# DMA transposes against TensorE transposes with token-major copies, half-width broadcast tiles and a deeper chunk order in a transformer block's forward and backward pass

## The chip, the cores and the metric

The kernel runs on one core of a Trainium2 chip. A core has a matrix engine (TensorE, PE in the profile; its weight loads are PEld), a vector engine (VectorE, DVE), a scalar engine (ScalarE, ACT), GpSimd (POOL) and a queue engine (SyncE, SP), each with an instruction stream of its own that is worked off in order. Engines wait for each other through semaphores. Sixteen DMA engines move data between DRAM and the core's memory; in this kernel the transfers are issued by SP (the hardware queue q1) and by POOL (the software queue q0). Matrix results land in PSUM, eight banks of 128 x 512 float32.

The metric is the device time of one execution in microseconds, median of several runs.

## The reference

One pre-norm transformer block, forward, and its gradients for the input and all weights. S = 2048 tokens, D = 512, F = 1792, 32 heads of 16, all in bfloat16.

```python
def _A_ref(x, wqkv, wo):                      # 32 heads, W = 8 keys each, dilation 2
    q, k, v = split((x @ wqkv))
    idx = pos[:, None] - arange(8)[None, :] * 2      # this token, 2 back, ... 14 back
    kg, vg = k[..., idx, :], v[..., idx, :]
    logits = einsum("bhsd,bhswd->bhsw", q, kg) * 16 ** -0.5   # masked where idx < 0
    o = einsum("bhsw,bhswd->bhsd", softmax(logits), vg)
    return merge_heads(o) @ wo
def _B_ref(x, w1, b1, w2, b2):
    return gelu_tanh(x @ w1 + b1) @ w2 + b2
h  = x + _A_ref(layernorm(x), wqkv, wo)
h2 = h + _B_ref(layernorm(h), w1, b1, w2, b2)
out, vjp = jax.vjp(f, x, wqkv, wo, w1, b1, w2, b2)
return (out, *vjp(grad_out))
```

## The kernel before

The tokens are worked in four chunks of 512 (`CH`). Most tiles are feature-major: features on the 128 partitions, tokens along the row. So a shift of keys by 2w tokens is an offset in the row, and one VectorE product over eight shifted views serves a group `g` of 128 features (8 heads).

**Forward** (lines 252 to 401). `f_qkv(c)` normalises a chunk, transposes it on TensorE (`to_T`: eight 128 x 128 transposes into one PSUM bank, one ScalarE copy out, line 219) and makes q, k, v, which also go to DRAM. `f_attn(c)` multiplies q with the eight shifted k (line 284, 128 x 4096), sums over a head by matmuls with the indicator `ind` (288), takes the softmax and writes it to DRAM as `attn_f` and `attn_b`. `f_o(c)` reads the softmax back, each head's row broadcast to its 16 feature partitions (`bcast`, 235 to 240: tile `bc`, 8 shifts x 512 tokens, half issued on SP and half on POOL), multiplies it with the shifted v (317), sums the shifts by matmuls with the identity (320) and stores the result `oT` to DRAM (322). `f_h(c)` applies wo and the second layernorm; `f_ffn(c)` makes u, the gelu through Square and Sigmoid on ScalarE (354, 358) and VectorE products, and the output; u, s and g go to DRAM (364). `f_wT` transposes wqkv and wo into DRAM scratch. The written order is attention of chunk c+1, then output, `f_h` and FFN of chunk c, then qkv of chunk c+2.

**Backward through the FFN** (410 to 527), chunks in the order 0, 3, 2, 1. w2T, w1T and each chunk's goutT are DMA transposes on SP straight from the inputs (411, 419, 427). `ffn_bwd` reloads u and s, multiplies the gradient by w2T (494), forms gh1 on VectorE (496), stores it feature-major (500), and takes it through w1T (508). Between its steps it draws from `gw2_gen`, which DMA-transposes g (456, four per 128 features) and multiplies it with grad_out for the gradient of w2 (459).

**Backward through attention** (531 to 682), chunks 3 to 0. `b_ga` makes the gradient of the attention output and of the weights, `b_sm` goes back through the softmax and writes it to DRAM as `gl_b`. `b_gv` broadcasts `attn_b` (595, four POOL transfers a tile), `b_gqk` broadcasts `gl_b` (609, 610, one transfer on SP and one on POOL); `gather` (582) sums the shifts on TensorE, copies out and stores the gradients of q, k, v feature-major (588). `b_gx` makes the input gradient and stores it from SP (628). `weights_gen`, drawn from in between, DMA-transposes gh1 (643) and oT (655) for the gradients of w1 and wo. At the end the gradients of q, k, v are DMA-transposed (693) for the gradient of wqkv (697).

A scheduler places the instructions: it takes the written order as a priority, fills an engine with whatever its model of times says is ready, and fixes each engine's order before the run. So the trace shows work of neighbouring steps interleaved. Tiles of one tag share a number of buffers (`bufs`), and a new tile waits until its buffer's last reader is done; a memory pool that opens after another has closed waits in the same way for the tiles that lay there.

Of the kernel before, what the change touches and what calls it, by code (L numbers as in the profile page):

```python
# [10 lines left out]
P = 128  # L11
# [6 lines left out]
H = 32  # L18
# [8 lines left out]
HB = CH + PAD  # L27

# [6 lines left out]
def kernel(  # L35
# [44 lines left out]
    psum = ctx.enter_context(tc.tile_pool(name="psum", bufs=2, space=PSUM))  # L80

    def acc(name, tag="accA"):
        return psum.tile([P, CH], F32, name=name, tag=tag)

    def ptile(name, tag="ptA"):
        return psum.tile([P, 8 * P], BF16, name=name, tag=tag, bufs=1)

    def ltile(name):
        return psum.tile([P, 2, W * H], F32, name=name, tag="lg", bufs=2)
# [35 lines left out]
    oT_d = [dram.tile([D, CH], BF16, name=f"oT_d{c}") for c in range(NC)]  # L125
    x_d = [dram.tile([F, CH], BF16, name=f"x_d{c}") for c in range(NC)]
    s_d = [dram.tile([F, CH], BF16, name=f"s_d{c}") for c in range(NC)]
    g_d = [dram.tile([F, CH], BF16, name=f"g_d{c}") for c in range(NC)]
    gh1_d = [dram.tile([F, CH], BF16, name=f"gh1_d{c}") for c in range(NC)]
    gq_d = [[dram.tile([D, CH], BF16, name=f"gq_d{s}_{c}") for c in range(NC)] for s in range(3)]  # L130
    wqkvT_d = dram.tile([NJ * P, D], BF16, name="wqkvT_d")
    woT_d = dram.tile([D, D], BF16, name="woT_d")

# [3 lines left out]
    def natural_rows(d_tile, g):  # L137
        b = d_tile[g * P:(g + 1) * P, :]
        rs = b.ap[-2][0]
        return _ap(b, [[rs, DH], [DH * rs, 8], [1, b.shape[-1]]])  # L140

    def over_w(a, n):
        return _ap(a, [a.ap[0], [0, W], [1, n]])

    def back_w(a, n):
        return _ap(a, [a.ap[0], [-DIL, W], [1, n]])
# [18 lines left out]
    for dc in range(DC):  # L165
        nat = fr.tile([P, 3 * D], BF16, name=f"nat{dc}", tag="pr", bufs=2)
# [68 lines left out]
    def bcast(out_t, d_t, g, n, parts):  # L235
        wq = W // len(parts)
        for i, e in enumerate(parts):
            b = d_t[8 * g:8 * g + 8, i * wq * n:(i + 1) * wq * n]
            e.dma_start(out=out_t[:, i * wq:(i + 1) * wq, :].rearrange("p w t -> p (w t)"),  # L239
                        in_=_ap(b, [[0, DH], [W * n, 8], [1, wq * n]]))  # L240
# [11 lines left out]
    def f_qkv(c):  # L252
# [8 lines left out]
        v = fr.tile([P, G, HB], BF16, name=f"v{c}", tag="v", bufs=2)  # L261
# [16 lines left out]

    def f_attn(c):
        q, k = qs[c], ks[c]  # L280
        lg = [ltile(f"lg{c}_{i}") for i in range(TC // 2)]
        for g in range(G):
            pr = fr.tile([P, W, CH], BF16, name=f"pr{c}_{g}", tag="pr", bufs=2)
# [27 lines left out]
    def f_o(c):  # L311
        v = vs[c]
        oT = fr.tile([P, G, CH], BF16, name=f"oT{c}", tag="oT", bufs=1)
        for g in range(G):
# [4 lines left out]
            for w in range(W):  # L319
                nc.tensor.matmul(ps[:], lhsT=ident[:], rhs=bc[:, w, :], start=(w == 0), stop=(w == W - 1))  # L320
# [412 lines left out]
```

## Time and profile before

| | us |
|---|---|
| median of 3 runs (1012.07 to 1033.3) | 1024.96 |
| profiled execution, whole | 1027.08 |
| its span on the core | 1025.3 |
| mean TensorE clock granted, share of full | 0.848 |
| forward attention's first broadcast product (line 317) at | 82 |
| first DMA transpose issued (w2T, line 411) at | 342 |
| last forward matmul (line 371) at | 434 |
| first matmul of attention's backward (line 547) at | 604 |
| last gx product (line 444) at | 962 |

Times in the profile count from the span's start. A row of a group gives line, engine, operation, written and read tiles, shape and count, then busy us and the mean ns of one, then the time in which the engine stood idle before these instructions and what ended most of it. A timeline row gives start, length, engine, line, operation and count, and in brackets the idle time before. SPq and POOLq are the two queues that issue transfers; a transfer's own time is its landing time. A row of stages gives the busy time of each engine in that stretch, the granted clock, the mean busy share of the sixteen DMA engines (it can pass 1 where transfers overlap) and GB/s. A busy TensorE includes the pipelined ends of matmuls.

### The profile page before, as it was taken

The numbers are of one execution on the slowest core, as the hardware profiler recorded it, in microseconds if no ns is written. First come the engines' busy times: TensorE is split into PE (matmuls) and PEld (weight loads), VectorE is DVE, ScalarE is ACT, GpSimd is POOL, SyncE is SP. The second block draws the span as 40 slices with busy tenths as digits, with TensorE's granted clock in tenths as the row PEclk, the third lists the DMA queues.
The fourth block names the chain that finished last, engine by engine and source line by source line (L and its number), as shares of the span: only waits on it lengthen the run. The fifth ranks groups of instructions, "written<-read, shape, count | busy, mean of one in ns | idle before, by whom it ended". The sixth has DMA issues, their size and how long they took to land.

```text
span 1025.3 us, 11102 instructions
## 1 busy us (share of the span) xinstructions
PE 723.7 (71%) x3999; PEld 328.7 (32%) x4066; DVE 537.0 (52%) x790; ACT 371.3 (36%) x527; POOL 302.4 (29%) x456
## 2 busy tenths in 40 slices
PE   2666578759668633759999876858676778667388
PEld 1433324324223211214444332423233324222133
DVE  5528473463543234547887875465255629637300
ACT  3552573564355344324554531213213122212211
POOL 6331351332225232434332214214213221422100
PEclk9878879779768866879999997889879788878789
DMA  8464753364277899998978769998799762856492
GB/s 300 145 182 137 215 226 119 98 212 155 73 202 245 182 171 149 211 250 233 273 169 210 179 181 155 218 210 248 143 169 188 185 181 76 247 153 158 130 215 68
DMA packets 173941, 186.20 MB, mean 182 GB/s; under 512 B 126205, under 2 KB 139390, under 8 KB 173886
## 3 DMA queue, kind: packets, MB, share of 16 engines
q0 software_dynamic: 38912, 125.69, 43.4%
q1 hardware_dynamic: 134974, 59.79, 32.4%
q8 instruction: 32, 0.52, 0.2%
q14 instruction: 23, 0.19, 0.1%
HBM read 93.00 MB, written 63.56 MB: 153 GB/s over the span
## 4 chain that ended last, share of the span: by engine, by line
PE 15%; DMA 13%; issue 9%; DVE 7%; SPq 5%; POOL 4%; ACT 3%; POOLq 0%; DVEq 0%; ACTq 0%
DMA bv<-attn_b 6%; DMA bg<-gl_b 4%; PE psq L697 4%; PE psa L582 3%; SPq L643 2%; PE psx L508 2%; PE psw L647 2%; PE psy L622 2%; SPq L693 1%; POOL bv L239 1%; DVE bh L609 1%; SPq L655 1%; DVE bv L595 1%; DMA bs<-s_d 1%; PE psgo L547 1%
## 5 line engine op out<-in xcount | busy, mean ns | idle before, releaser
L582 PEld LDWEIGHTS <-ident 128*128 128x128 bf16 x384 | 39.9, 107 | 142.4 <-DVE bv L595 45.3
L350 PE MATMUL psf<-ln2T,w 128*128 128x512 bf16 x218 | 64.9, 445 | 24.2 <-ACT u L352 23.5
L595 DVE TENSOR_TENSOR bv<-bv,go 128x4224 bf16<-128x4224 bf16 x16 | 37.6, 2355 | 69.5 <-DMA bv<-attn_b 63.6
L317 DVE TENSOR_TENSOR bc<-bc,v 128x4096 bf16<-128x4096 bf16 x16 | 36.6, 2288 | 63.5 <-DMA bc<-attn_f 63.5
L582 PE MATMUL psa<-bv,ident 128*128 128x512 bf16 x126 | 38.2, 458 | 44.8 <-DVE bv L595 42.5
L494 PE MATMUL psg<-goutT,w2T 128*128 128x512 bf16 x218 | 53.8, 382 | 21.2 <-DMA goutT<-in_grad_out_dram 19.7
L459 PE MATMUL psw<-gout,gtm 128*128 128x512 bf16 x220 | 55.3, 384 | 11.5 <-ACT o L373 6.5
L274 PE MATMUL psq<-ln1T,wqkv 128*128 128x512 bf16 x188 | 50.1, 410 | 18.3 <-ACT k L276 17.0
L368 PE MATMUL ps<-w,g 128*128 128x512 bf16 x217 | 56.4, 408 | 8.5 <-DVE g L360 5.3
L582 PE MATMUL psa<-bh,ident 128*128 128x512 bf16 x123 | 37.0, 445 | 31.1 <-DVE bh L609 30.5
L622 PE MATMUL psy<-wqkvT,gt 128*128 128x512 bf16 x188 | 47.9, 412 | 14.8 <-DVE lua L443 14.3
L697 PE MATMUL psq<-gqt,ln1a 128*128 128x512 bf16 x188 | 44.6, 396 | 18.9 <-DMA ln1a<-ln_d 16.4
L239 POOL DMA_DIRECT2D bv<-attn_b x64 | 33.9, 538 | 80.5 <-PE psa L582 76.3
L508 PE MATMUL psx<-w1T,gh 128*128 128x512 bf16 x220 | 52.5, 394 | 5.0 <-DVE gb1p L496 4.6
L320 PE MATMUL pso<-bc,ident 128*128 128x512 bf16 x122 | 38.4, 459 | 24.8 <-DVE bc L317 24.3
L609 DVE TENSOR_TENSOR bh<-bg,bk 128x4096 bf16<-128x4096 bf16 x16 | 36.4, 2288 | 35.7 <-DMA bg<-gl_b 35.7
L284 DVE TENSOR_TENSOR pr<-q,k 128x4096 bf16<-128x4096 bf16 x16 | 36.2, 2294 | 35.5 <-PE lg L288 27.3
L588 POOL DMA_DIRECT2D gq_d<-gt x48 | 26.0, 541 | 96.2 <-ACT gt L585 77.1
L647 PE MATMUL psw<-h1tm,ln2a 128*128 128x512 bf16 (+1 forms) x249 | 53.8, 355 | 0.5 <-issue 0.2
L352 ACT ACTIVATE u<-psf,b1c 128x512 bf16<-128x512 f32 x56 | 36.5, 683 | 36.3 <-PE psf L350 19.4
L585 ACT ACTIVATE gt<-psa 128x512 bf16<-128x512 f32 x32 | 19.1, 597 | 84.0 <-PE psa L582 84.0
L350 PEld LDWEIGHTS <-w 128*128 128x128 bf16 x224 | 24.8, 112 | 70.1 <-issue 53.8
(183 smaller groups left out, 1443.6 us busy)
## 6 DMA issues: line engine op xcount, KB each, us to landing
bv<-attn_b POOLq DMA_DIRECT2D x64, 264.0 KB, 5.7
bg<-gl_b POOLq DMA_DIRECT2D x16, 528.0 KB, 10.5
bg<-gl_b SPq DMA_DIRECT2D x16, 528.0 KB, 12.6
bc<-attn_f SPq DMA_DIRECT2D x16, 512.0 KB, 7.9
bc<-attn_f POOLq DMA_DIRECT2D x16, 512.0 KB, 10.4
x_d<-u POOLq DMA_DIRECT2D x28, 256.0 KB, 9.0
s_d<-s POOLq DMA_DIRECT2D x28, 256.0 KB, 2.9
g_d<-g POOLq DMA_DIRECT2D x28, 256.0 KB, 2.8
```

Source lines behind the costliest of these rows:

```text
L274: nc.tensor.matmul(ps[:], lhsT=wqkv[:, dc, jt * P:(jt + 1) * P], rhs=ln1T[:, dc, :], start=(dc == 0), stop=(dc == DC - 1))
L350: nc.tensor.matmul(ps[:], lhsT=w1[:, dc, ft * P:(ft + 1) * P], rhs=ln2T[:, dc, :], start=(dc == 0), stop=(dc == DC - 1))
L368: nc.tensor.matmul(ps[:], lhsT=gs[ft // 2][:, ft % 2, j * P:(j + 1) * P], rhs=w2[:, ft, :], start=(ft == 0), stop=False)
L459: nc.tensor.matmul(ps[:], lhsT=gtm[:, t // TC, t % TC, :], rhs=gout[t // TC][:, t % TC, :], start=(t == 0), stop=(t == NT - 1))
L494: nc.tensor.matmul(ps[:], lhsT=w2T[:, dc, ft * P:(ft + 1) * P], rhs=gT[:, dc, :], start=(dc == 0), stop=(dc == DC - 1))
L508: nc.tensor.matmul(ps[:], lhsT=gh1[ft // 2][:, ft % 2, j * P:(j + 1) * P], rhs=w1T[:, ft, :], start=(ft == 0), stop=(ft == FT - 1))
L582: nc.tensor.matmul(ps[:], lhsT=ident[:], rhs=src[:, w, o:o + CH], start=(w == 0), stop=(w == W - 1))
L595: nc.vector.tensor_tensor(out=bc[:], in0=bc[:], in1=over_w(gos[c][:, g, :], HB), op=ALU.mult)
L609: nc.vector.tensor_tensor(out=pr[:], in0=bc[:, :, 0:CH], in1=back_w(k[:, g, PAD:HB], CH), op=ALU.mult)
L622: nc.tensor.matmul(ps[:], lhsT=gts[c][sel][:, g, j * P:(j + 1) * P], rhs=wqkvT[:, sel * G + g, :], start=(n == 0), stop=(n == NJ - 1))
L647: nc.tensor.matmul(ps[:, 0:nf * P], lhsT=ln2a[:, t // TC, t % TC, dc * P:(dc + 1) * P], rhs=tmx[:, t // TC, t % TC, 0:nf * P], start=(t == ...
L697: nc.tensor.matmul(ps[:], lhsT=ln1a[:, t // TC, t % TC, dc * P:(dc + 1) * P], rhs=gqt[:, t // TC, t % TC, :], start=(t == NT - 1), stop=(t ...
```

## The change

No DMA transpose is left; all plain transfers keep their bytes.

- **Weights.** `f_wT` now also transposes w1 and w2 on TensorE in the forward pass, into DRAM scratch, and w1T, w2T are plain loads from there.
- **grad_out** is loaded token-major, and goutT made by `to_T`.
- **g** is one DRAM tensor with a row of 2048 tokens for each feature; `gw2_gen` loads 128 rows with one transfer and transposes them on TensorE (16 transposes, 2 copies).
- **gh1** is transposed on TensorE in `ffn_bwd` as it is made (8 transposes, 1 copy for 256 features) and stored token-major; `weights_gen` loads it plainly.
- **oT and the gradients of q, k, v** are transposed by the new `to_tm`, whose ScalarE copy also puts the features back in their natural order, and stored token-major, one transfer a chunk in place of four; the loads are plain, on POOL.
- **Tiles of four shifts** (`WH`) replace those of eight in all products of attention; three buffers become five or six of half the size; every broadcast goes out on SP.
- **Order.** The forward order is written out by hand, with attention up to two chunks ahead of its output and the last two FFNs at the end. The gelu's square moves from ScalarE to VectorE. u keeps 3 buffers, s goes from 3 to 2, g from 9 to 8, v from 2 to 3, ln2T from 1 to 2.
- **PSUM** is split into three pools in turn; in the two backward ones the weight gradients have one bank (`gw`) in place of two, and psg and psx have two each of their own.

```diff
+WH = W // 2
 def over_w(a, n):
-    return _ap(a, [a.ap[0], [0, W], [1, n]])
+    return _ap(a, [a.ap[0], [0, WH], [1, n]])
-def back_w(a, n):
-    return _ap(a, [a.ap[0], [-DIL, W], [1, n]])
+def back_w(a, n, w0):
+    return _ap(a, [a.ap[0], [-DIL, WH], [1, n]], off=-DIL * w0)
...
-    def bcast(out_t, d_t, g, n, parts):
-        wq = W // len(parts)
-        for i, e in enumerate(parts):
...
+    def bcast(eng, out_t, d_t, g, n, w0):
+        b = d_t[8 * g:8 * g + 8, w0 * n:(w0 + WH) * n]
+        eng.dma_start(out=out_t[:].rearrange("p w t -> p (w t)"), in_=_ap(b, [[0, DH], [W * n, 8], [1, WH * n]]))
+
+    def to_tm(src, dst, nm, tag):
+        for j2 in range(TC // 2):
+            pt = ptile(f"pt{nm}{j2}", tag)
+            for i in range(2):
+                for g in range(G):
+                    o = (i * G + g) * P
+                    j = 2 * j2 + i
+                    nc.tensor.transpose(pt[:, o:o + P], src[:, g, j * P:(j + 1) * P], ident[:])
+            o_ap = dst[:, 2 * j2:2 * j2 + 2, :]
+            nc.scalar.copy(out=_ap(o_ap, [o_ap.ap[0], [P, 8], [DH, 8], [1, DH]]),
+                           in_=_ap(pt[:], [pt[:].ap[0], [P, 8], [1, 8], [8, DH]]))
...
         for g in range(G):
-            bc = fr.tile([P, W, CH], BF16, name=f"bc{c}_{g}", tag="bc", bufs=3)
-            bcast(bc, attn_f[c], g, CH, (sync, pq))
...
             ps = acc(f"pso{c}_{g}")
+            for w0 in (0, WH):
+                bc = fr.tile([P, WH, CH], BF16, name=f"bc{c}_{g}{w0}", tag="bc", bufs=6)
+                bcast(sync, bc, attn_f[c], g, CH, w0)
+                nc.vector.tensor_tensor(out=bc[:], in0=bc[:], in1=back_w(v[:, g, PAD:HB], CH, w0), op=ALU.mult)
...
-            pq.dma_start(out=natural_rows(oT_d[c], g), in_=oT[:, g, :])
...
+        otm = fr.tile([P, TC, D], BF16, name=f"otm{c}", tag="otm", bufs=1)
+        to_tm(oT, otm, f"o{c}", "ptB")
+        pq.dma_start(out=tm(otm_d[c * CH:(c + 1) * CH, :]), in_=otm[:])
...
-            nc.scalar.activation(out=z[:], in_=u[:], func=ACT.Square)
+            nc.vector.tensor_tensor(out=z[:], in0=u[:], in1=u[:], op=ALU.mult)
...
-    f_wT()
-    for c in range(NC):
-        if c + 1 < NC:
-            f_attn(c + 1)
-        f_o(c)
-        f_h(c)
-        f_ffn(c)
-        if c + 2 < NC:
-            load_x(c + 2)
-            f_qkv(c + 2)
+    f_wT(wqkv, DC, wqkvT_d, NJ)
+    f_wT(wo, G, woT_d, DC)
+    f_attn(1)
+    load_x(2)
+    f_qkv(2)
+    f_wT(w1, DC, w1T_d, FT)
+    f_wT(w2, FT, w2T_d, DC)
+    f_o(0)
+    f_h(0)
+    f_attn(2)
+    f_o(1)
+    f_h(1)
+    f_ffn(0)
+    load_x(3)
+    f_qkv(3)
+    f_attn(3)
+    f_o(2)
+    f_h(2)
+    f_ffn(1)
+    f_o(3)
+    f_h(3)
+    f_ffn(2)
+    f_ffn(3)
+    psum[0].release()
...
-    sync.dma_start_transpose(out=w2T[:], in_=B_w2[:, :])
+    pq.dma_start(out=w2T[:], in_=w2T_d[:, :].rearrange("(dc p) f -> p dc f", p=P))
...
-            sync.dma_start_transpose(out=goutT[c][:], in_=gof[c * CH:(c + 1) * CH, :])
+            to_T(gout[c], goutT[c], f"e{c}", "ptA")
-    sync.dma_start_transpose(out=w1T[:], in_=B_w1[:, :])
+    pq.dma_start(out=w1T[:], in_=w1T_d[:, :].rearrange("(ft p) d -> p ft d", p=P))
...
-            for c in range(NC):
-                sync.dma_start_transpose(out=gtm[:, c, :, :], in_=g_d[c][ft * P:(ft + 1) * P, :])
-            ps = acc(f"psw2{ft}", "accB")
+            sync.dma_start(out=gr[:], in_=g_d[ft * P:(ft + 1) * P, :])
+            for t0 in range(0, NT, 8):
+                pt = ptile(f"ptg{ft}_{t0}", "ptB")
+                for k_ in range(8):
+                    nc.tensor.transpose(pt[:, k_ * P:(k_ + 1) * P], gr[:, (t0 + k_) * P:(t0 + k_ + 1) * P], ident[:])
+                nc.scalar.copy(out=gtm[:, t0:t0 + 8, :], in_=pt[:].rearrange("p (t f) -> p t f", t=8))
+            ps = acc(f"psw2{ft}", "gw", 1)
...
-            pq.dma_start(out=dd.rearrange("(i p) t -> p i t", p=P), in_=t1[:])
+            pt = ptile(f"pth{c}_{f2}", "ptA")
+            for j in range(TC):
+                for k2 in range(2):
+                    o = (j * 2 + k2) * P
+                    nc.tensor.transpose(pt[:, o:o + P], t1[:, k2, j * P:(j + 1) * P], ident[:])
+            nc.scalar.copy(out=th[:], in_=pt[:].rearrange("p (j f) -> p j f", j=TC))
+            pq.dma_start(out=dd.rearrange("(j p) f -> p j f", p=P), in_=th[:])
...
-            bcast(bc, attn_b[c], g, HB, (pq, pq, pq, pq))
+                bcast(sync, bc, attn_b[c], g, HB, w0)
...
-        pq.dma_start(out=natural_rows(gq_d[sel][c], g), in_=dst)
+    def put_tm(c, sel):
+        t_ = bp.tile([P, TC, D], BF16, name=f"gqt{sel}_{c}", tag="gqt", bufs=2)
+        to_tm(gts[c][sel], t_, f"q{c}{sel}", "ptA")
+        pq.dma_start(out=tm(gq_d[sel][c][:, :]), in_=t_[:])
...
-                sync.dma_start_transpose(out=tmx[:, c, :, 0:nf * P], in_=gh1_d[c][f0 * P:(f0 + nf) * P, :])
+            pq.dma_start(out=tmx[:, :, 0:nf * P], in_=tm(h1tm_d[:, f0 * P:(f0 + nf) * P]))
...
-            sync.dma_start_transpose(out=gqt[:, c, :, :], in_=gq_d[sel][c][:, :])
+            pq.dma_start(out=gqt[:, c, :, :], in_=tm(gq_d[sel][c][:, :]))
```

More of the change, by code (lines that the diff above doesn't have):

```diff
@@ L277, in f_qkv, with logits @@
             chunk_io(dst[:, :, o:o + CH], d_t, PAD + c * CH, CH, True, pq)
+    def logits(lg, pr, g, w0):
+        for j in range(TC):
+            for w in range(WH):
+                col = 32 * (w0 + w) + 8 * g
+                nc.tensor.matmul(lg[j // 2][:, j % 2, col:col + 8], lhsT=pr[:, w, j * P:(j + 1) * P],
+                                 rhs=ind[:], start=True, stop=True)
     def f_attn(c):
@@ L674 @@
             b_sm(c - 1)
[L675 removed]
+        b_gqk(c)
         take(wg, 1)
[L677 removed]
+        b_gx(c)
         take(wg, 1)
```

203 lines of the change are left out of this document (101 added, 102 removed).

## The prediction

> **What bounds the kernel now.** I read the page's totals and its DMA queues first, then the span cut into stages, then the waits, then the timelines of SP and TensorE where the waits are longest.
>
> ```profile
> span 1025.3 us, 11102 instructions
> PE 723.7 (71%) x3999; PEld 328.7 (32%) x4066; DVE 537.0 (52%) x790; ACT 371.3 (36%) x527; POOL 302.4 (29%) x456
> ...
> q0 software_dynamic: 38912, 125.69, 43.4%
> q1 hardware_dynamic: 134974, 59.79, 32.4%
> ```
>
> No engine fills the span. The two DMA queues together are busy 75.8% of it, and the packets of q1 (SP's queue, which holds every transpose) are the slow ones. From the shapes, the transposes read 28.8 MB: both FFN weights 3.7, grad_out 2.1, g and gh1 7.3 each, gq 6.3, oT 2.1. The other 31.0 MB of q1 at q0's rate (125.69 MB in 43.4% of 1025.3 = 445 us, 282 GB/s) take 110 us; q1 took 332, so the transposes cost about 222 us of all sixteen engines, 130 GB/s, an estimate that puts queueing on them too.
>
> Cut at four places that I chose from the timeline (chunk 3's second layernorm is transposed; the pass back through chunk 0's FFN is over; attention's backward begins; the last gx), the stages are:
>
> ```profile
> core 0: us, PE busy (x) PEld busy (x) DVE busy (x) ACT busy (x) POOL busy (x), PEclk, DMA share, GB/s
> 0.00:350.00 350.00, 238.08 (x1481) 113.03 (x1502) 173.54 (x257) 165.58 (x220) 121.10 (x179) 0.83 0.58 178
> 350.00:456.00 106.00, 51.75 (x190) 19.76 (x193) 41.15 (x85) 41.25 (x49) 34.08 (x48) 0.76 1.15 190
> 456.00:604.00 148.00, 139.94 (x617) 60.69 (x630) 116.91 (x268) 74.22 (x101) 51.06 (x74) 0.98 0.84 208
> 604.00:962.00 358.00, 249.38 (x1526) 115.94 (x1551) 204.80 (x182) 83.25 (x146) 93.19 (x152) 0.84 0.80 176
> 962.00:1025.30 63.30, 44.56 (x188) 19.32 (x192) 0.61 (x1) 7.03 (x12) 3.01 (x4) 0.85 0.74 160
> ```
>
> Call them A to E. C alone is bound by TensorE (140 of 148 us, clock 0.98). B has every engine below half and the DMA at 1.15; D runs the DMA at 0.80 while VectorE waits. The list of waits (total us, times, longest) says for what:
>
> ```profile
> DVE bv L595 <- DMA bv<-attn_b: 63.6, 10, 17.6
> DVE bc L317 <- DMA bc<-attn_f: 63.5, 8, 15.0
> DVE bh L609 <- DMA bg<-gl_b: 35.7, 7, 12.5
> PE pso L320 <- DVE bc L317: 24.3, 6, 7.8
> ```
>
> The broadcast tiles are late: 63.5 us forward, 99.3 us backward. Beside them stand the transposes, and SP's timeline (start, us) shows how long they hold its queue:
>
> ```profile
> 341.68 7.08 SPq L411 DMA_TRANSPOSE w2T<-in_B_w_dram  x1
> 348.80 14.97 SPq L419 DMA_TRANSPOSE goutT<-in_grad_out_dram  x1
> 364.30 31.18 SPq L427 DMA_TRANSPOSE w1T<-in_B_w_dram  x1
> ...
> 610.14 48.94 SPq L643 DMA_TRANSPOSE h1tm<-gh_d  x8
> ...
> 963.06 26.43 SPq L693 DMA_TRANSPOSE gqt<-gq_d  x8
> ```
>
> **The change, stage by stage.** Four prices serve throughout: two lines of TensorE's timeline, three of the costliest groups (busy us, mean ns), and the last link of the chain.
>
> ```profile
> 588.87 0.61 PE L217 MATMUL ptc<-ident,gh 128*128 128x128 bf16 x8
> 590.62 0.22 PE L217 MATMUL ptc<-ident,gh 128*128 128x128 bf16 x1 [1.14 <-ACT ghT L219]
> ...
> L219 ACT COPY ln1T<-pta 128x1024 bf16<-128x1024 bf16 x8 | 8.1, 1013 | 8.1 <-PE pta L217 7.9
> L317 DVE TENSOR_TENSOR bc<-bc,v 128x4096 bf16<-128x4096 bf16 x16 | 36.6, 2288 | 63.5 <-DMA bc<-attn_f 63.5
> L484 DVE TENSOR_TENSOR by<-by,bu 128x1024 bf16<-128x1024 bf16 x28 | 19.4, 691 | 0.9
> 1010.34 10.74 PE psq L697 x49
> ```
>
> A group of eight PE transposes is 0.61 us of TensorE and a 1.01 us ScalarE copy; where the next group wants the same PSUM bank at once, TensorE stands 1.14 us. I count 111 new groups: 15 for w1 and w2, 8 for otm, 8 for goutT, 28 for gtm, 28 for h1, 24 for gq. A full-clock matmul of 512 columns is 10.74/49 = 0.219 us. A product over four shifts (2048 columns), interpolated between 1024 (0.691) and 4096 (2.288), is 1.223 us, so two cost 0.16 us more than one of eight shifts.
>
> *A, 350 us.* Attention now runs up to two chunks ahead of its output, so a chunk's broadcasts can be fetched early.
>
> ```profile
> 110.00:197.00 87.00, 63.63 (x382) 29.00 (x386) 42.47 (x58) 43.52 (x61) 28.80 (x42) 0.83 0.50 160
> L354 ACT ACTIVATE z<-u 128x1024 bf16<-128x1024 bf16 x28 | 29.6, 1058 | 0.2
> L175 ACT COPY wqkv<-nat 128x1536 bf16<-128x1536 bf16 x2 | 5.9, 2952 | 6.6 <-DMA nat<-in_A_wqkv_dram 6.6
> ```
>
> One chunk lasts 87 us here (the first row, from one second layernorm to the next) with no engine above 64. The gain lies between TensorE's own wait (24.3) and VectorE's (63.5); I take the middle, 44.
>
> The square moves from ScalarE (29.6 us) to VectorE (28 at about 0.691 = 19.3); both have room, so I take nothing (bounds -10 and +19). The 23 groups add 14 us of TensorE and 23 us of copies in a stage where TensorE is idle 112 us; a regrouping copy may cost twice a plain one (L175 pays 1.9 ns a column, L219 1.0), 8 us more. I let 8 us show (bounds 0 and 23 x 1.75 = 40). The extra DMA (7.3 MB for the weights' scratch, 26 us at 282 GB/s) lies under a DMA share of 0.58. The 16 pairs of products and as many of pr add 5 us to VectorE, in its idle half. A: -36.
>
> *B, 106 us.* Two waits of TensorE, one of ScalarE, and a weight load of the size of w2T:
>
> ```profile
> 374.05 1.01 PE L494 MATMUL psg<-goutT,w2T 128*128 128x512 bf16 x2 [19.67 <-DMA goutT<-in_grad_out_dram]
> ...
> 403.50 3.57 PE L350 MATMUL psf<-ln2T,w 128*128 128x512 bf16 x8 [15.92 <-ACT u L352]
> ...
> ACT u L352 <- DMA x_d<-u: 13.4, 1, 13.4
> ...
> w<-in_B_w_dram POOLq DMA_DIRECT2D x2, 1792.0 KB, 11.2
> ```
>
> The second wait is the third in disguise: chunk 3's FFN cannot reuse u because its store crawls beside the transposes. All three go: w2T and w1T arrive by plain loads of 1.8 MB (the two FFN weights of that size landed in 11.2 us), and since f_ffn(2) and f_ffn(3) now follow the last f_h, the right-hand memory is free two FFNs earlier, 2 x 120 matmuls x 0.219 = 53 us. What is late next is TensorE itself: 120 matmuls of the FFN, 56 of the first psg and 16 of psb are 192 x 0.219 = 42 us. I take 50, so -56 (bounds -64, and 0 if POOL issues those loads only behind the last stores of x, s and g).
>
> *C, 148 us.* It gets dearer. 616 matmuls are 135 us; 64 groups add 64 x 0.61 = 39 us to TensorE, of which overlapping starts give back some, and 65 us to ScalarE (74 becomes 139). What vanishes is a wait of 4.6 us for gtm:
>
> ```profile
> L459 PE MATMUL psw<-gout,gtm 128*128 128x512 bf16 x220 | 55.3, 384 | 11.5 <-ACT o L373 6.5 <-DMA gtm<-g_d 4.6
> ```
>
> Two new waits stand in TensorE's order: h1's transposes wait for VectorE's product with y (L496), and psw, now with one bank, for ScalarE's copy of the last one; the next psg or psw queues behind either. Bounds: +25, and 64 x 1.75 = +112 if no other matmul is placed between the groups of one bank. The timeline there alternates psw, psg and psx, so there is filler, and I stay near the lower: +35.
>
> *D, 358 us.*
>
> ```profile
> 749.97 3.59 PE L582 MATMUL psa<-bv,ident 128*128 128x512 bf16 x8 [13.90 <-DVE bv L595]
> ...
> 685.64 1.89 PE L582 MATMUL psa<-bg,ident 128*128 128x512 bf16 x8
> ...
> SPq L628 <- DVE gx L444: 82.4, 13, 27.7
> ...
> POOL gq_d L588 <- ACT gt L585: 77.1, 21, 16.8
> ```
>
> All broadcasts go to SP, which no longer issues transposes but still carries the gx stores; behind those, waiting for VectorE, now stand the next chunk's bv tiles. Until now bv stood on POOL behind the gq stores, which wait for ScalarE: one such wait against the other, priced at nothing (bounds -30, +40). In transfer time (KB each, median us to landing) SP and POOL are alike:
>
> ```profile
> bg<-gl_b POOLq DMA_DIRECT2D x16, 528.0 KB, 10.5
> bg<-gl_b SPq DMA_DIRECT2D x16, 528.0 KB, 12.6
> ```
>
> Of the 99.3 us on bv and bg I let 60 go: each chunk keeps one landing of about 10 us after its softmax, which is the other 40. Every long wait also cools TensorE (eight matmuls take 3.59 us behind a wait, 1.89 without); eight fewer are 8 x 1.7 = 14. Against: 64 pairs of products, +10 on VectorE, which with TensorE is the fullest engine here. The 24 gq groups lie in the idle time of TensorE and ScalarE (83 of 358 us busy). D: -64 (bounds -110, +10).
>
> *E, 63 us.*
>
> ```profile
> L697 PE MATMUL psq<-gqt,ln1a 128*128 128x512 bf16 x188 | 44.6, 396 | 18.9 <-DMA ln1a<-ln_d 16.4 <-DMA gqt<-gq_d 2.3
> ```
>
> 192 matmuls are 42 us and stay. The start waits 16.4 us for ln1a, issued by POOL once the memory is free, and the gqt loads now queue behind it there instead of running beside it. I take -5 (bounds -12, +6).
>
> Sum: -36 - 56 + 35 - 64 - 5 = -126. The profiled execution took 1027.08 us for its span of 1025.3, 2 us above the median of the runs, 1024.96. From the median: 899, said as 900.
>
> On the transposes' price a page speaks against the change. The Trainium skill, DMA: Bandwidth & Descriptors, section on latency and other measured facts, gives a DMA transpose 261 GB/s in the awkward case and 350 to 400 in the contiguous one. By that 28.8 MB are 110 us, no more than the plain traffic that replaces them, and the DMA would not be relieved. The trace's 130 GB/s decides for me; by the page the gains of B, D and E would fall away, which is the third rival below.
>
> **The rivals.** *Copies in line (15%).* C is the one dense stage, ptA and ptB have one bank each. If every group there waits for its copy, C grows 112 instead of 35: 977. For it: the 1.14 us above. Against: filler matmuls between.
>
> *SP holds the broadcasts (12%).* bv and bg wait as long as now, behind gx and weight stores; D gains nothing: 900 + 64 = 964. For it: SP's 82.4 us on gx. Against: five half tiles can be in flight.
>
> *Loads are no cheaper (7%).* The token-major transfers take as long as the transposes did. A -36, C +35, D +10, the rest unchanged: 1034, no change.
>
> *Slower (5%).* All 111 groups stand open at 0.61 + 1.14 us: 194 us, against the gains of A, B, D and E without their eviction term, 169: 1050. It decides from about 1.7 us a group, that is only if nearly all are open, while A and D have idle TensorE.
>
> *Better (8%).* The engines' loads bind: D falls by its other bound: about 855.
>
> **The numbers.** 53% stands on the forecast, its own range 855 to 945. Within 2%, about what a measurement of this kernel tells from no change, means 1004 to 1045. Range of 8 in 10: 845 to 980, which takes in the first two rivals and the better one. Faster 0.88, same 0.07, slower 0.05.
>
> **What would show it.** B: w2T and goutT ready before chunk 3's FFN ends, no TensorE wait above 8 us there; wrong if POOL's loads come late. C: 175 to 195 us at a clock near 1.00; wrong if waits on the copies sum above 30 us. D: waits on bv and bg below 50 us together, DMA share below 0.75. q1 would carry some 70 MB and still take less than 30% of the span. Wrong altogether if the broadcast waits stay at their 163 us.

## The result and the profile after

The changed kernel takes 925.93 us (925.74 to 929.76) against 1024.96 (1012.07 to 1033.3): 0.910 of the time before, interval 0.896 to 0.925. The profiled execution's span is 924.2 us, 101 less than before. Times here and below are medians of all runs, while ratios and their intervals (in brackets) are of the fast runs alone, those at most 1.5% above the fastest; beside four kernels (all DMA transposes back, the same with eight-shift tiles, the queues alone, the late weight transposes) only three of seven runs of the kernel before were fast, so that these four ratios rest on little and their verdict stays unclear.

First the totals and the two DMA queues of the changed kernel, then its stages. They are cut to match A to E. The second row begins 16 us after the last forward matmul, the time of the 72 matmuls that the prediction still counts to B; before, C began 22 us after it, so that some 6 us between B and C hang on this choice. The columns are those of the stage table in the prediction.

```profile
span 924.2 us, 12961 instructions
PE 759.3 (82%) x4946; PEld 373.9 (40%) x4946; DVE 560.8 (61%) x914; ACT 442.3 (48%) x608; POOL 252.8 (27%) x342
...
q0 software_dynamic: 34144, 114.41, 37.5%
q1 hardware_dynamic: 30558, 72.63, 28.1%
```

```profile
0.00:389.00 389.00, 290.22 (x1903) 142.88 (x1904) 220.56 (x371) 197.57 (x262) 144.14 (x200) 0.88 0.65 214
389.00:569.00 180.00, 170.93 (x1108) 86.87 (x1106) 133.28 (x304) 133.44 (x168) 55.36 (x75) 1.00 0.52 163
569.00:864.50 295.50, 253.35 (x1750) 124.75 (x1747) 206.94 (x240) 103.72 (x166) 41.37 (x53) 0.93 0.79 220
864.50:924.20 59.70, 44.83 (x194) 19.42 (x192) 0.00 (x0) 7.61 (x13) 11.92 (x16) 0.88 0.47 172
```

A and B together went from 456 to 389 (-67, forecast -92), C from 148 to 180 (+32, forecast +35), D from 358 to 295.5 (-62.5, forecast -64), E from 63.3 to 59.7 (-3.6, forecast -5). The list of VectorE's waits on the broadcasts (us in total, times, longest) has lost more than half of its 163 us:

```profile
DVE bc L330 <- DMA bc<-attn_f: 36.3, 14, 8.3
DVE bv L638 <- DMA bv<-attn_b: 27.0, 14, 4.8
...
DVE bh L657 <- DMA bg<-gl_b: 6.9, 7, 1.5
```

q1 carries 72.6 MB in 28.1% of the span, D has 34 us of waits on bv and bg, and C runs at a clock of 1.00 in 180 us: of the signs that the prediction asked for in the profile only D's DMA share, 0.79 instead of below 0.75, is missing. The experiments show that the shorter waits in B and D have another cause than the one it gave.

### The profile page after: what moved, and what is told of

It reads as the page before. It is cut to its first block, busy times and chain, and to the rows that moved or that the text cites. A ratio compares the mean times of both kernels' runs of the same rounds, so it can differ in the third digit from the quotient of the medians.

```text
span 924.2 us, 12961 instructions
## 1 busy us (share of the span) xinstructions
PE 759.3 (82%) x4946; PEld 373.9 (40%) x4946; DVE 560.8 (61%) x914; ACT 442.3 (48%) x608; POOL 252.8 (27%) x342
## 3 DMA queue, kind: packets, MB, share of 16 engines
q1 hardware_dynamic: 30558, 72.63, 28.1%
## 4 chain that ended last, share of the span: by engine, by line
PE 29%; DVE 14%; issue 13%; DMA 12%; ACT 6%; POOL 4%; ACTq 0%; DVEq 0%; POOLq 0%
DMA bv<-attn_b 5%; PE psq L747 5%; PE psw L698 4%; DMA bg<-gl_b 4%; PE psy L674 4%; PE psw L496 3%; PE psg L531 2%; PE psk L624 1%; PE psx L552 1%; PE psv L624 1%; DVE bv L638 1%; DVE bg L658 1%; ACT bu L522 1%; PE pswo L709 1%; DVE by L523 1%
## 5 line engine op out<-in xcount | busy, mean ns | idle before, releaser
L330 DVE TENSOR_TENSOR bc<-bc,v 128x2048 bf16<-128x2048 bf16 x32 | 38.8, 1222 | 36.4 <-DMA bc<-attn_f 36.3
L600 DVE TENSOR_TENSOR bp<-go,bv 128x2048 bf16<-128x2048 bf16 x32 | 36.8, 1221 | 36.3 <-ACT go L595 36.3
L299 DVE TENSOR_TENSOR pr<-q,k 128x2048 bf16<-128x2048 bf16 x32 | 37.3, 1219 | 35.0 <-ACT q L283 30.5
L638 DVE TENSOR_TENSOR bv<-bv,go 128x2112 bf16<-128x2112 bf16 x32 | 39.7, 1253 | 29.9 <-DMA bv<-attn_b 27.0
L747 PE MATMUL psq<-gqa,ln1a 128*128 128x512 bf16 x192 | 44.5, 397 | 11.3 <-DMA gqa<-gq_d 11.3
L402 ACT COPY wT<-ptw 128x1024 bf16<-128x1024 bf16 (+1 forms) x23 | 22.4, 975 | 44.8 <-DMA w1T_d<-wT 15.3
L657 DVE TENSOR_TENSOR bh<-bg,bk 128x2048 bf16<-128x2048 bf16 x32 | 38.5, 1218 | 8.4 <-DMA bg<-gl_b 6.9
L372 ACT ACTIVATE s<-z 128x1024 bf16<-128x1024 bf16 x28 | 29.4, 1054 | 28.9 <-DVE z L370 16.3
L533 DVE CUSTOM_DVE_ANT_0 gh<-psg,by 128x512 bf16<-128x512 f32 x56 | 37.3, 686 | 8.2 <-PE psg L531 7.3
L624 PE MATMUL psv<-bv,ident 128*128 128x512 bf16 x128 | 34.7, 415 | 7.6 <-DVE bv L638 7.6
```

Of the source, the lines that this page charges most:

```text
L330: nc.vector.tensor_tensor(out=bc[:], in0=bc[:], in1=back_w(v[:, g, PAD:HB], CH, w0), op=ALU.mult)
L624: nc.tensor.matmul(ps[:], lhsT=ident[:], rhs=src[:, w, o:o + CH], start=(w0 + w == 0), stop=(w0 + w == W - 1))
L638: nc.vector.tensor_tensor(out=bc[:], in0=bc[:], in1=over_w(gos[c][:, g, :], HB), op=ALU.mult)
L747: nc.tensor.matmul(ps[:], lhsT=ln1a[:, t // TC, t % TC, dc * P:(dc + 1) * P], rhs=gqt[:, t // TC, t % TC, :], start=(t == NT - 1), stop=(t ...
```

## The experiments

Each kernel below ran beside the kernel before on one chip; "ratio" is its time over that. For orientation the stages of the kernels that matter (us, from the profiled executions: up to the last forward matmul; the FFN's backward pass; the attention's, up to the last gx; the rest). A row is one execution, and the runs of one kernel below differ by 5 to 20 us in all, so a difference of some 10 us between two rows is an indication and no more:

| kernel | forward | FFN backward | attention backward | tail |
|---|---|---|---|---|
| before | 434 | 170 | 358 | 63.3 |
| the change | 373 | 196 | 295.5 | 59.7 |
| all DMA transposes back | 377.4 | 176.6 | 294.6 | 61.5 |
| the same, order of before | 372.9 | 180.2 | 295.9 | 61.9 |
| all DMA transposes back, eight-shift tiles and queues of before | 399 | 190 | 285 | 62.9 |
| before with the PSUM banks split | 420 | 181.5 | 280.5 | 61.9 |
| the change with one PSUM pool | 374.8 | 199 | 334.2 | 58.7 |
| the change with g, oT, gq by DMA | 364.5 | 189.8 | 284.2 | 62.7 |

**One group of transposes back at a time.** The theory was that of the prediction: the DMA transposes are the cost, and SP's queue behind them. First the weights (w1T in the same way as w2T, the two `f_wT` calls for them gone) and grad_out.

```diff
...
-    pq.dma_start(out=w2T[:], in_=w2T_d[:, :].rearrange("(dc p) f -> p dc f", p=P))
+    sync.dma_start_transpose(out=w2T[:], in_=B_w2[:, :])
...
-            to_T(gout[c], goutT[c], f"e{c}", "ptA")
+            sync.dma_start_transpose(out=goutT[c][:], in_=gof[c * CH:(c + 1) * CH, :])
...
```

> The changed kernel, but w2T, w1T and goutT are DMA transposes from the inputs again, and the forward pass transposes only wqkv and wo. Theory (the DMA transposes were what the wait between forward and backward was made of): the last forward matmul, 373 us now, moves out by 25 to 45 us or TensorE waits 15 us or more for w2T or goutT, while the start gains some 10 us from the missing weight transposes; 945 to 965 us in all. Rival (the new order with the last two FFNs at the end covers these loads, however they are made): within 10 us of 926, and no wait above 8 us there.

Measured: 931.27 us (925.28 to 938.12), ratio 0.913 [0.905, 0.921], not told apart from the change and below the 945 to 965 of the theory. The forward part grew by 7 us, no more, in a profile of the slowest of the four runs. Then g alone, in place of one load, 16 transposes and 2 copies for 128 features:

```diff
-            sync.dma_start(out=gr[:], in_=g_d[ft * P:(ft + 1) * P, :])
...
+            for c in range(NC):
+                sync.dma_start_transpose(out=gtm[:, c * TC:(c + 1) * TC, :], in_=g_d[ft * P:(ft + 1) * P, c * CH:(c + 1) * CH])
```

> The changed kernel, but g is transposed by 56 DMA transposes on SP again. Theory (the FFN's backward is bound by TensorE, each group of eight transposes costs its own 0.45 to 0.61 us there, and a DMA transpose in that stage had room): 28 groups fewer take 10 to 17 us off the stage, 909 to 916 us. Rival one (the groups hide behind ScalarE and VectorE): 926 within 5. Rival two (a DMA transpose crawls and makes TensorE wait for gtm): 935 to 950, with waits on gtm of 15 us or more.

Measured: 919.16 us (913.26 to 919.92), ratio 0.899 [0.893, 0.906]. The FFN's backward pass lasts 187 us instead of 196, so g looks better left to the DMA; the intervals of the two ratios overlap. Then gh1 alone, stored feature-major as before:

```diff
-            pt = ptile(f"pth{c}_{f2}", "ptA")
...
+            pq.dma_start(out=gh1_d[c][2 * f2 * P:(2 * f2 + 2) * P, :].rearrange("(i p) t -> p i t", p=P), in_=t1[:])
...
-            pq.dma_start(out=tmx[:, :, 0:nf * P], in_=tm(h1tm_d[:, f0 * P:(f0 + nf) * P]))
+            for c in range(NC):
+                sync.dma_start_transpose(out=tmx[:, c * TC:(c + 1) * TC, 0:nf * P], in_=gh1_d[c][f0 * P:(f0 + nf) * P, :])
```

> The changed kernel, but gh1 is stored feature-major and transposed by 16 DMA transposes on SP in attention's backward again; its 28 groups on TensorE are gone. Theory (these transposes hold SP and the DMA engines while the broadcast tiles are wanted): the FFN's backward shortens by 10 to 17 us, attention's backward (295 us now) lengthens by 35 to 60; 945 to 970 us. Rival (half-width tiles and the longer prefetch made attention's backward faster, the transposes were beside it): attention's backward stays within 10 us of 295, 905 to 920 us.

Measured: 933.83 us (929.94 to 936.98), ratio 0.916 [0.909, 0.923], between the ranges of theory and rival. Here the theory has a true core. The FFN's backward pass gains 10 us (557 less 371), but the attention's lasts 312 instead of 295.5, and VectorE's waits on bv grow from 27.0 to 37.6 us. SP's timeline of this kernel shows the eight transposes at its start:

```profile
556.38 33.67 SPq L688 DMA_TRANSPOSE h1tm<-gh_d  x8
```

**The order.** The hand-written forward order back to that of before, all else as changed.

```diff
-    f_attn(1)
-    load_x(2)
-    f_qkv(2)
...
+    for c in range(NC):
+        if c + 1 < NC:
+            f_attn(c + 1)
+        f_o(c)
+        f_h(c)
+        f_ffn(c)
+        if c + 2 < NC:
+            load_x(c + 2)
+            f_qkv(c + 2)
```

> The changed kernel with the forward order of before (attention of chunk c+1, output, f_h, FFN of chunk c, qkv of c+2), the weight transposes at the same place. Theory of the prediction (the deeper order is worth some 44 us of broadcast waits): 955 to 975 us, waits on bc back above 50 us. Rival (the deeper order loses at the start, where the first output waits for another attention, another qkv and the weights, what it gains in the middle): 916 to 936 us.

Measured: 931.44 us (927.96 to 934.12), ratio 0.913 [0.907, 0.919]: against 0.910 for the change, nothing that these intervals tell apart. The last forward matmul even comes 12 us earlier (361 against 373), and the FFN's backward pass gives it back. VectorE's waits on bc are 26.4 us with the order of before (36.3 in the change), not above 50 as the theory had it.

**All DMA transposes back.** Weights, grad_out, g, gh1, oT and gq, with the feature-major stores; tiles, queues of the broadcasts, order, PSUM pools and the square stay as changed. Beside the three edits above:

```diff
-        put_tm(c, 2)
+            pq.dma_start(out=natural_rows(gq_d[2][c], g), in_=gts[c][2][:, g, :])
...
-            pq.dma_start(out=gqt[:, c, :, :], in_=tm(gq_d[sel][c][:, :]))
+            sync.dma_start_transpose(out=gqt[:, c, :, :], in_=gq_d[sel][c][:, :])
...
-        pq.dma_start(out=otm[:], in_=tm(otm_d[:, :]))
+        for c in range(NC):
+            sync.dma_start_transpose(out=otm[:, c * TC:(c + 1) * TC, :], in_=oT_d[c][:, :])
```

> The changed kernel with every transpose of the kernel before back at once (w2T, w1T, goutT, g, gh1, oT, and the gradients of q, k, v with their four stores a chunk), but with the half-width tiles, all broadcasts on SP, the new order, the PSUM pools and the square on VectorE kept. Three of these parts alone cost +5, -7 and +8 us. Theory (each alone finds room, together they fill SP's queue and the DMA engines again): 950 to 980 us, attention's backward above 320 us. Rival (the parts add, and the gain lies elsewhere, in the tiles and queues): 930 to 940 us.

Measured: 909.62 us (903.18 to 921.59), ratio 0.890 [0.880, 0.900]. This is the run that fells the theory: with every transpose on the DMA again the kernel is faster than the change by the medians, and below the ranges of theory and rival. (On the same chip the change with a later place for two of its transposes, shown below, took 923.34 to 927.99 us.) Its totals, its queues, and VectorE's waits on the broadcasts:

```profile
span 910.1 us, 11178 instructions
...
PE 699.3 (77%) x3998; PEld 323.4 (36%) x4066; DVE 556.6 (61%) x914; ACT 341.1 (37%) x497; POOL 252.3 (28%) x360
...
q1 hardware_dynamic: 144190, 94.14, 45.0%
q0 software_dynamic: 29184, 91.34, 32.5%
```

```profile
DVE bv L622 <- DMA bv<-attn_b: 34.3, 12, 7.2
...
DVE bc L335 <- DMA bc<-attn_f: 26.4, 9, 7.9
...
DVE bh L641 <- DMA bg<-gl_b: 12.2, 8, 4.9
```

The transposes cost DMA time here too. At the rate of the changed kernel's q1 (72.63 MB in 28.1% of 924.2, 280 GB/s) the 65.3 MB of plain traffic take 233 us of the 410 (45.0% of 910.1), and 176 are left for 28.8 MB. But the broadcasts wait 73 us in all, hardly more than the 70 of the changed kernel. Here, then, the DMA time of the transposes did not make the tile that is needed next late. In the transition the same holds; SP's timeline and TensorE's longest waits there (270 to 420 us):

```profile
276.67 14.62 SPq L446 DMA_TRANSPOSE w2T<-in_B_w_dram  x1
291.46 8.52 SPq L455 DMA_TRANSPOSE goutT<-in_grad_out_dram  x1
300.23 20.53 SPq L460 DMA_TRANSPOSE w1T<-in_B_w_dram  x1
```

```profile
PE psf L367 <- ACT o L390: 12.4, 1, 12.4
PE psf L367 <- ACT u L369: 11.8, 6, 7.7
PE psw L492 <- ACT gb L484: 7.6, 1, 7.6
```

The three transposes take 44 us (53 before), and none of TensorE's waits is for them: there is forward work until 377.

**What is left without the half-width tiles.** This kernel has eight-shift tiles, the queues of before and one ln2T buffer as well; of the change, only the order, the PSUM pools and the square remain (with the smaller edits of buffers and stores).

```diff
...
-            for w0 in (0, WH):
+            for w0 in (0,):
-                bc = bl.tile([P, WH, HB], BF16, name=f"bv{c}_{g}{w0}", tag="bc", bufs=5)
-                bcast(sync, bc, attn_b[c], g, HB, w0)
+                bc = bl.tile([P, W, HB], BF16, name=f"bv{c}_{g}{w0}", tag="bc", bufs=3)
+                bcast((pq, pq, pq, pq), bc, attn_b[c], g, HB, w0)
```

> The kernel of u5_all_dmaT with eight-shift tiles and the queues of before as well (half of bc and bg on POOL, bv in four pieces on POOL) and one ln2T buffer: what is left of the change is the order, the PSUM pools and the square. Theory (transposes and late broadcasts are one jam, so tiles and queues matter little once the transposes are there): within 15 us of u5_all_dmaT. Rival (the half-width tiles on SP are where attention's backward got faster): 25 us or more above u5_all_dmaT, waits on bv and bg back near 100 us.

Measured: 937.68 us (934.54 to 947.92), ratio 0.922 [0.908, 0.935]. So tiles and queue, with the ln2T buffer, are worth some 28 us, in the forward part (399 against 377) and the FFN's (190 against 177). In the attention's backward pass they cost some 10 us together (295 against 285), and VectorE's waits on bv and bg, 19.8 and 21.1 us, stay far from the 100 that the rival expected. And that pass is at 285 us with all transposes, wide tiles and old queues back: what shortened it from 358 had to be in the little that was left.

**Two small ones.** The queues alone, four-shift tiles kept: attn_b on POOL, of attn_f and gl_b the second half of the shifts on POOL too.

```diff
...
-                bcast(sync, bc, attn_b[c], g, HB, w0)
+                bcast(pq, bc, attn_b[c], g, HB, w0)
...
-                bcast(sync, bc, gl_b[c], g, HB, w0)
+                bcast(sync if w0 == 0 else pq, bc, gl_b[c], g, HB, w0)
```

> The changed kernel with its half-width tiles, but the queues of before: of bc and bg one half on SP and one on POOL, bv all on POOL. Theory (the move to SP swaps one wait for another, priced at nothing): 926 within 8. Rival (POOL's queue, with the stores that wait for ScalarE ahead of bv, held the broadcasts): 940 to 960 us with waits on bv above 50 us.

Measured: 930.64 us (928.27 to 940.36), ratio 0.915 [0.905, 0.925], the same as the change within these intervals. Its stage of the attention's backward pass is 9 us shorter (the change has 295.5); the forward part and the FFN's, 380.5 and 199.5 us, are 11 us longer.

```profile
580.00:866.80 286.80, 244.82 (x1706) 121.89 (x1732) 206.03 (x240) 103.68 (x166) 64.27 (x95) 0.96 0.81 226
```

The other one moves the transposes of w1 and w2 behind the first FFN.

```diff
-    f_wT(w1, DC, w1T_d, FT)
-    f_wT(w2, FT, w2T_d, DC)
     f_o(0)
...
     f_ffn(0)
+    f_wT(w1, DC, w1T_d, FT)
+    f_wT(w2, FT, w2T_d, DC)
```

> The changed kernel with the transposes of w1 and w2 written behind the first FFN instead of ahead of the first output. Theory (they delay the first f_h, which starts at 128 us now and at 97 before, because each waits for the store of the one before it): the first f_h comes 10 to 20 us sooner and the whole takes 908 to 920 us. Rival (the second attention and third qkv ahead of it are what delays it, or the start is made up later): 926 within 6.

Measured: 925.03 us (923.34 to 927.99), ratio 0.908 [0.901, 0.915]: also the same. The weights' transposes sit ahead of the first output, but written behind the first FFN they give the same time.

**The PSUM banks.** New theory, from a row of the kernel before that the prediction had left aside. POOL's waits there, for the issue of the broadcasts (tile, then whom it waits for):

```profile
POOL bv L239 <- PE psa L582: 76.3, 7, 18.8
POOL bg L239 <- PE psa L582: 41.6, 5, 17.5
```

POOL could not start these transfers, because the tile they go to was still being read by the gathers `psa` on TensorE. The tiles were late because the transfers began late, not because they ran slowly. TensorE's timeline of before shows why the gathers were late:

```profile
705.85 5.34 PE L622 MATMUL psy<-wqkvT,gt 128*128 128x512 bf16 x24
711.02 1.03 PE L647 MATMUL psw<-h1tm,ln2a 128*128 128x512 bf16 x4
711.89 0.61 PE L217 MATMUL ptc<-ident,gh 128*128 128x128 bf16 x8
...
714.30 1.67 PE L647 MATMUL psw<-h1tm,ln2a 128*128 128x512 bf16 x7
718.52 6.75 PE L622 MATMUL psy<-wqkvT,gt 128*128 128x512 bf16 x24 [2.54 <-DVE lua L443]
725.11 1.03 PE L647 MATMUL psw<-h1tm,ln2a 128*128 128x512 bf16 x4
726.09 1.89 PE L582 MATMUL psa<-bv,ident 128*128 128x512 bf16 x8
```

`psy` (the input gradient, 12 matmuls a tile) and `psa` share two banks. Two `psy` tiles are filled at 705.85, each is emptied by a chain of one ScalarE and two VectorE reads of the bank, and until 718.5 only work on other banks (`psw`, transposes) runs; then come two more. No gather runs between 705.85 and 726. The change gives `psy`, too, two banks of its own (`gx`), which the list of the change does not say. One kernel takes that away from the change, one adds it alone to the kernel before.

```diff
...
-                ps = acc(f"psg{c}_{ft}", "gg", 2)
+                ps = acc(f"psg{c}_{ft}")
...
-    psum[0].release()
-    psum[0] = pool("ps_b2", 1, space=PSUM)
...
-            ps = acc(f"psy{c}_{j}", "gx", 2)
+            ps = acc(f"psy{c}_{j}")
...
-                ps = acc(f"psw1{f0}_{dc}", "gw", 1)
+                ps = acc(f"psw1{f0}_{dc}", "accB")
```

> The changed kernel with one part undone: the accumulators of the two backward passes share the banks of before again (one PSUM pool; psg, psx, psgo, psv, psq, psk and psy on the same two banks, psw and pswo on two others). PE transposes, half-width tiles, queues and order stay. Theory A (the split of the PSUM banks carries the gain of the backward attention, because psy's slow eviction no longer holds the banks that the gathers want): the backward attention goes from 295 us to some 345-360, total 975-990. Theory B (broadcasts in time and no transposes carry it, as the prediction had it): unchanged, 920-935.

Measured: 968.75 us (963.35 to 974.51), ratio 0.951 [0.945, 0.958], 43 us more than the change. The stage of the attention's backward pass, and VectorE's waits on bv:

```profile
573.80:908.00 334.20, 261.96 (x1742) 126.98 (x1770) 208.68 (x240) 107.82 (x170) 42.38 (x54) 0.92 0.72 195
```

```profile
DVE bv L634 <- DMA bv<-attn_b: 50.5, 20, 5.3
```

The pass grows by 39 us, the other stages by 4 together. At 334 us it stays a little below the expected 345 to 360, and the total below the 975 to 990: each wait is shorter (5.3 us at most, 17.6 before), perhaps because the five half-width tiles cover part of the delay, which no run shows.

The reverse, the kernel before with the opposite edit and nothing else:

```diff
+    psum[0].release()
+    psum[0] = pool("ps_b2", 1, space=PSUM)
...
-            ps = acc(f"psy{c}_{j}")
+            ps = acc(f"psy{c}_{j}", "gx", 2)
...
-                ps = acc(f"psw1{f0}_{dc}", "accB")
+                ps = acc(f"psw1{f0}_{dc}", "gw", 1)
```

> The kernel before with only the split of the PSUM banks added (a pool per pass, psg, psx and psy on pairs of their own, psw on one); DMA transposes, eight-shift tiles, queues and order are those of before. Theory A: the backward attention falls from 358 us to 290-310, the waits on bv and bg (99 us) fall below 55, and the total is 955-975. Theory B: within 15 us of before, 1010-1035.

Measured: 958.7 us (945.8 to 965.45; the profiled execution is the fastest of them), ratio 0.933 [0.924, 0.943]. Two thirds of the whole gain by the medians (61 of 99 us), three quarters by the ratios (0.067 of 0.090), come with tags and pools of PSUM alone. The two profiled executions differ by 81 us, so what their stages say of the split is in sum 13 to 20 us too much. The attention's backward pass, POOL's and VectorE's waits, and TensorE's timeline of this kernel:

```profile
601.50:882.00 280.50, 230.54 (x1521) 111.00 (x1546) 200.33 (x175) 81.27 (x142) 89.35 (x150) 0.93 0.91 224
```

```profile
POOL bg L239 <- PE psa L586: 11.6, 6, 3.4
POOL bv L239 <- PE psa L586: 7.4, 4, 3.2
```

```profile
DVE bv L599 <- DMA bv<-attn_b: 16.4, 8, 7.4
DVE bh L613 <- DMA bg<-gl_b: 15.2, 6, 6.4
```

```profile
706.41 1.02 PE L586 MATMUL psa<-bv,ident 128*128 128x512 bf16 x3 [1.89 <-DMA bv<-attn_b]
707.27 2.75 PE L626 MATMUL psy<-wqkvT,gt 128*128 128x512 bf16 x12
709.86 1.68 PE L586 MATMUL psa<-bv,ident 128*128 128x512 bf16 x7
711.38 2.75 PE L626 MATMUL psy<-wqkvT,gt 128*128 128x512 bf16 x12
713.96 2.97 PE L586 MATMUL psa<-bv,ident 128*128 128x512 bf16 x13
```

`psy` and the gathers now alternate. POOL's two waits fall from 118 to 19 us, VectorE's on bv and bg from 99 to 32, and the pass from 358 to 280.5, with all transposes on SP, eight-shift tiles and the queues of before. Of all kernels here only the two without the split, before and the change with one pool, have a pass above 330 us; the others have 280 to 313. The split is one edit in several parts: that it works through `psy`'s own pair is read from these timelines, and that pair alone was not run. By the Trainium skill, Perfetto Trace Analysis, section Optimizing Tensor Performance, independent groups of matmuls should rotate through different PSUM banks, so that the emptying of one overlaps the matmuls of the next; these two kernels agree, with 61 and 43 us.

**Order and transposes as substitutes.** One doubt was left: the order had been undone only where no DMA transpose was there to be hidden. This is the kernel with all DMA transposes, with the loop of the order run in place of the hand-written list.

```diff
-    f_attn(1)
-    load_x(2)
-    f_qkv(2)
...
+    for c in range(NC):
+        if c + 1 < NC:
+            f_attn(c + 1)
...
```

> The changed kernel with all DMA transposes back (909.6 us measured) and the forward order of before. If the order and the removal of the transposes are two ways to the same end, the start of the FFN's backward pass (no DMA transpose of w1 and w2 in time), the transposes show again when the order is gone too: 945-975. If the order is worth as little here as beside the PE transposes (5 us): 910-920.

Measured: 904.05 us (902.24 to 912.64), ratio 0.889 [0.883, 0.895]. The order is worth nothing here either. With the order run above it makes a second pair that differs only in where the transposes are done, with the stores that belong to that: 0.889 [0.883, 0.895] by DMA, 0.913 [0.907, 0.919] on TensorE, intervals that do not meet (those of the first pair, 0.890 [0.880, 0.900] and 0.910 [0.896, 0.925], overlap a little). By these two pairs the move to TensorE costs some 2 to 3% of the kernel.

**A mixture.** The weights, grad_out and gh1 on TensorE, g, oT and gq on the DMA.

```diff
-            sync.dma_start(out=gr[:], in_=g_d[ft * P:(ft + 1) * P, :])
...
+            for c in range(NC):
+                sync.dma_start_transpose(out=gtm[:, c * TC:(c + 1) * TC, :], in_=g_d[ft * P:(ft + 1) * P, c * CH:(c + 1) * CH])
...
-            pq.dma_start(out=gqt[:, c, :, :], in_=tm(gq_d[sel][c][:, :]))
+            sync.dma_start_transpose(out=gqt[:, c, :, :], in_=gq_d[sel][c][:, :])
```

> A mixture that ought to beat both: the changed kernel with g, oT and gq transposed by DMA again, while the weights, grad_out and h1 stay on TensorE. From the single runs: g by DMA -7, oT and gq by DMA about -16 (what is left of -16 in all after +5 for the weights, +8 for h1 and -7 for g: -22, less some overlap), so 895-910. If the single effects don't add: 910-925.

Measured: 900.11 us (896.42 to 903.01), ratio 0.883 [0.878, 0.889]: below both kernels; from the two with all transposes by DMA (0.889 and 0.890) it is not told apart for certain. Its stages:

```profile
0.00:364.50 364.50, 269.20 (x1701) 132.12 (x1727) 209.26 (x348) 179.21 (x240) 143.40 (x205) 0.86 0.66 218
364.50:554.30 189.80, 173.98 (x978) 82.86 (x997) 139.96 (x326) 119.43 (x153) 60.71 (x82) 0.99 0.68 175
554.30:838.50 284.20, 239.25 (x1521) 113.62 (x1546) 205.73 (x239) 80.80 (x142) 56.66 (x87) 0.92 0.83 228
838.50:901.20 62.70, 45.92 (x195) 19.82 (x196) 0.71 (x2) 7.61 (x13) 3.02 (x4) 0.89 0.71 164
```

Against all transposes by DMA, the attention's backward pass is 10 us shorter (gh1's eight transposes no longer stand at its start); against the change, 11 us shorter (gq's 24 groups no longer stand in TensorE's order; gq alone was not run). In the change these two cancel.

## Why the prediction was right, and where its reasons were not

The direction and the range held: 925.93 lies in 845 to 980 and in the forecast's own 855 to 945. The likeliest value, 900, was 26 us low. Stage by stage the forecast was close in C, D and E, but D's closeness is luck: the gain came from another edit.

- **D, -64, measured -62.5: right in size, wrong in cause.** The step that failed is the first one, "Beside them stand the transposes": it read late broadcasts and a busy DMA (0.80 of the engines) as late because of a busy DMA. With the banks alone split, the same stage runs the DMA at 0.91 and 280.5 us. The prediction let 60 us of these waits go, and tied that gain to the transposes; the waits did go (99.3 to 33.9), but they went with `psy`'s banks, an edit that it did not cost in D at all (of the banks it costed only psw's single one, in C). The move of gq that it priced at nothing, in idle time of TensorE and ScalarE, costs some 11 us by the mixture, and gh1's transposes by DMA, the one place where its reason holds, cost some 10 to 17.
- **One queue's wait against the other, nothing: right in the sum.** In D it costs 9 us, inside its bounds, and the forward and FFN parts give it back: 930.64 with the queues of before, no difference that can be told. Since the tiles and the queue together cost D some 10, little is left of the 10 us given to its half-width products.
- **A and B, -92, measured -67: this is the missing part.** The order's 44 us in A were not there; undone, with either kind of transpose, it costs nothing that can be told. B's wait for goutT did go, but not because the transposes did: with all of them kept none of TensorE's waits there is for one, and the longest is 12.4 us (19.67 before). With the banks alone split there is none either: `psg`, which before started at 374 and had to wait for goutT, starts behind the last forward matmul, at 421. What shortened the forward part is told only in pieces: the split of the banks brings its end from 434 to 420, half-width tiles with SP's queue and a second ln2T buffer from 399 to 377. The remaining 21 us between 420 and 399 lie between the order, the square on VectorE and the edits of buffers; no run took the square alone, and since the order gave nothing in two other places, the square is the likelier, by argument only.
- **C, +35, measured +32: right in size, in two parts.** Counted from the last forward matmul the FFN's pass grew by 26 us (170 to 196). With all DMA transposes it has 176.6, 7 above before, for the other edits (the split of the banks alone gives 181.5, as no `psg` runs ahead of the last forward matmul any more); the TensorE transposes add the other 19, which the single runs split into 9 for g and 10 for gh1. That is 0.34 us a group (19/56), even below the lower bound of 25/64 = 0.39 that the prediction stayed near. *Copies in line* did not come: TensorE's waits on the copies in C sum to a few us.
- **E, -5, measured -3.6: right in size.** With all DMA transposes E is 61.5 us, so about half of the gain is theirs, by one profile each.
- **Loads are no cheaper.** The time of this rival was wrong (1034), its statement was nearer the truth than the forecast's: taking the transposes off the DMA relieved no path but that of gh1, and cost more than that on TensorE. Its page, the Trainium skill, DMA: Bandwidth & Descriptors, section Latency and other measured facts, gives a transpose 261 GB/s or more. The packets of the run with all transposes are still slower than that (28.8 MB in 176 us, 163 GB/s, an estimate that holds queueing), so the page's rate is not shown; but B and D kept their gains, which the prediction had tied to that rate.

The extra time of a regrouping copy, which the working of A put at up to 8 us, does not exist; the line of the changed kernel's code that does it shows both of its uses at the price of a plain copy (1013 ns in the prediction; here min/median/max ns):

```profile
L246 ACT COPY gqt<-ptq x24: 990/1010/1012, 606.9 to 855.9; 128x1024 bf16<-128x1024 bf16 x24
...
L246 ACT COPY otm<-pto x8: 1012/1018/1042, 150.0 to 297.0; 128x1024 bf16<-128x1024 bf16 x8
```

## What to carry to other kernels

Where an engine waits for a transfer, look at when the transfer was issued before looking at how fast it ran: a queue that waits for a buffer passes the blame back to the buffer's last reader, here to matmuls that shared their PSUM banks with a slowly emptied accumulator. A busy DMA beside a late tile is no proof that the one makes the other late; put the DMA work back alone and see. And when several edits arrive together, undo each on its own and also add the smallest alone to the old kernel: here fewer than twenty lines of PSUM pools and tags gave at least two thirds of the gain, and the move of the transposes took some of it back.

## What the runs showed of the hardware

The stage with the split banks moved 224 GB/s at a DMA share of 0.91 where the kernel before moved 176 at 0.80, with the same bytes (63 MB): 0.80 was no ceiling. In the same stage TensorE's granted clock rose from 0.84 to 0.93, and its busy time fell from 249 to 231 us for the same matmuls: with the gaps closed, they also ran faster. A ScalarE copy out of PSUM that regroups single bf16 elements from a stride of eight took 1.01 us for 1024 columns, as long as one in order (1.01 us).
